# Gated MLP of a transformer block on one core: z1 and z2 made in three column chunks instead of four, and the last block of the output product in two matmuls instead of three

## The chip, the cores and the metric

The kernel runs on one core of one Trainium2 chip. The metric is the time of one execution on the device in microseconds (us); where several runs are given, their median. The profile is one execution of the same program taken by the hardware profiler.

## The reference, cut to what matters

```python
x = A_x                                            # (1, 2048, 512)
h = x + attention(layernorm(x), wqkv, wo)          # 32 heads of 16
z = gelu(layernorm(h) @ w_in)                      # (1, 2048, 1376), tanh form of gelu
z1 = z[..., :688]
z2 = layernorm(z[..., 688:])
g = einsum("ts,bsf->btf", w_sp, z2) + b_sp         # w_sp is 2048 x 2048
out = h + (z1 * g) @ w_out                         # w_out is 688 x 512
```

All inputs and outputs are float32.

## The kernel before, in words

**Precision.** Most matrix products are made of numbers split in two parts: hi is the number rounded to the TensorE's fp32r format, lo is the rest. `mm3` (L92) makes one product block from three matmuls: hi by hi (L93), hi by lo (L94), lo by hi (L95). In each the first operand after the accumulator is stationary (its weight load is PEld in the profile), the second is streamed, one column after another.

**Stages.** (1) Projections and row maxima of the scores, then attention, to about 1407 us of the span. (2) The middle stage, L931 to L972, one row block of 128 rows after another, in the order `h_rows`. (3) The spatial product `w_sp @ z2` with its quarters combined to save products, first half at L1018 to L1126. (4) The last stage, L1196 to L1262, two row blocks in each round `p`: the rest of the spatial product, the gate, and the product with `w_out`.

**The order of work.** From L866 on every engine runs its instructions in the order in which the program writes them; nothing is moved by a scheduler. An instruction waits for the semaphores of what it reads and for the release of what it overwrites.

**A row block of the middle stage (rows `row[k]`).** PE first makes h of row block k+2 (`make_h`, 12 matmuls of 512 columns, L614), then turns the normalised h of row block k+1 (`turn`, four transposes, L882). Then it makes z of row block k: `make_z(sb, i, c)` (L891) makes one chunk of 344 columns in an accumulator of one PSUM bank (five of them rotate) with four `mm3` over the contraction, so 12 matmuls with the transposed h as stationary operand and `w_in` streamed; ScalarE then applies gelu from the accumulator to z (L898). There are four chunks: z2 left, z2 right, z1 left, z1 right (L951, L954, L960, L961). Between them stand `split_o` (L953: the attention output for row block k+3 is split, ScalarE and VectorE), the statistics of z2 (L956, after the second chunk), and the normalised h of row block k+2 (L959, ScalarE, behind the second chunk's gelu). `gate_z` (L900) stores z1 (L904), finishes the statistics, normalises z2 (L909), stores it (L910), and for the second half of the rows forms the sums that stage 3 needs on GpSimd (on VectorE for the last row block). The z1 tile has one buffer, the z2 tile five.

**The product with `w_out` in the last stage.** The gated rows `pr` (128 x 688) must be transposed to serve as stationary operand. 688 is five blocks of 128 and one of 48. `FB` (L39) starts the sixth block at column 560, so it overlaps the fifth; the rows of its weights that were already used are zero (the memset at L1106 and the loading DMA at L1107). `Out.turn` (L1171) makes six transposes (L1176) into PSUM and splits them in two groups of three blocks: hi on ScalarE (L85), lo on VectorE (L90). `Out.multiply` (L1180) then runs `mm3` for each of the six blocks: 18 matmuls of 512 columns for each of the 16 row blocks. The weights `wu` are split at L1128 to L1135.

Of the kernel before, what the change touches and what calls it, by code (L numbers as in the profile page):

```python
# [8 lines left out]
F32 = mybir.dt.float32  # L9
F32R = mybir.dt.float32r  # L10
BF = mybir.dt.bfloat16
I32 = mybir.dt.int32
AF = mybir.ActivationFunctionType
# [5 lines left out]
P = 128  # L19
# [16 lines left out]
FIRST = 1  # L36
RG = 64
VW = DH + 1
FB = [min(i * P, FH - P) for i in range(6)]  # L39
FC = FH // 2  # L40
PITCH = FC + 8
LOW = -3.0e38


@with_exitstack
def block_kernel(ctx: ExitStack, tc: tile.TileContext, x, wqkv, wo, w_in, w_sp4, b_sp, w_out, out):
# [820 lines left out]
    with ExitStack() as mid:  # L867
        m2 = mid.enter_context(tc.tile_pool(name="mid_2", bufs=2))
        zs, zst = {}, {}
        hT = wc.tile([P, 2, 2, DB, P], F32R, name="hT", tag="w2")  # L870
        ph = mid.enter_context(tc.tile_pool(name="mid_ph", bufs=1, space=PSUM))
        pt = mid.enter_context(tc.tile_pool(name="mid_pt", bufs=2, space=PSUM))
        ps = mid.enter_context(tc.tile_pool(name="mid_ps", bufs=5, space=PSUM))

        turned = [0]

        def turn(sb):

            hn = hns.pop(sb)
            tp = pt.tile([P, DB, P], F32, name="tp")  # L880
            for d in range(DB):
                nc.tensor.transpose(tp[:, d, :], hn[:, d * P:(d + 1) * P], ident)  # L882
            hTs[sb] = [hT[:, i, turned[0] % 2] for i in range(2)]
            turned[0] += 1
            split(hTs[sb][0], hTs[sb][1], tp, "act")

        def new_z(sb):
            zs[sb] = [m2.tile([P, FH], F32, name=f"z{i}", bufs=1 + 4 * i) for i in range(2)]
            zst[sb] = m2.tile([P, 2, 6], F32, name="zst")

        def make_z(sb, i, c):  # L891

            hT, f = hTs[sb], slice(i * FH + c * FC, i * FH + (c + 1) * FC)
            acc = ps.tile([P, 512], F32, name="acc")
            for d in range(DB):
                mm3(acc[:, :FC], hT[0][:, d, :], hT[1][:, d, :],
                    wi2[0][:, d, f], wi2[1][:, d, f], d == 0, d == DB - 1)
            nc.scalar.activation(zs[sb][i][:, c * FC:(c + 1) * FC], acc[:, :FC], AF.Gelu_apprx_tanh)  # L898

        def gate_z(sb, meanwhile):  # L900

            z = zs.pop(sb)
            rows = slice(sb * P, (sb + 1) * P)
            nc.scalar.dma_start(z_scr[0][rows, :], z[0])  # L904
            mv = m2.tile([P, 2], F32, name="zmv")
            nc.vector.bn_aggr(mv, zst.pop(sb))
            rs = rstd_of(m2, mv[:, 1:2], 1)
            nb = minus_mean(m2, mv, rs)
            nc.scalar.activation(z[1], z[1], AF.Identity, bias=nb, scale=rs)  # L909
            nc.scalar.dma_start(z_scr[1][rows, :], z[1])  # L910
            zs[sb] = z[1]
            meanwhile()
            if sb < HB:
                return

            k = sb - HB
            el = "pool" if k < HB - 1 else None
            e = nc.gpsimd if el else nc.vector
            (b11, b12), (b21, b22) = ((t[:, :FC], t[:, FC:]) for t in (zs.pop(k), zs.pop(sb)))
            t2 = m2.tile([P, FC], F32, name="t2", bufs=1)  # L920
            e.tensor_sub(b11, b12, b11)
            e.tensor_sub(b12, b22, b12)
            e.tensor_sub(t2, b22, b11)
            put_t = lambda n, t: parts(T[n][0][:, k, :], T[n][1][:, k, :], t, el, el)
            put_t("t3", b12)
            put_t("t2", t2)
            put_t("t1", b11)
            e.tensor_sub(b11, b21, t2)
            put_t("n4", b11)

        w = [Slot(wc, f"w{i}") for i in range(3)]  # L931
        row = dict(enumerate(h_rows))
        turn(row[0])
        for k in range(NB):
            sb, new = row[k], row.get(k + 2)
            if new is not None:
                make_h(new, (ph if k else ps).tile([P, 512], F32, name="acc"))
            if k + 1 < NB:
                turn(row[k + 1])
            if new is not None:  # L940
                mv, rs = scale_h(new)
                nb = minus_mean(e2, mv, rs)
            if k == NB - 3:
                s3 = difference(a11, a21, nc.gpsimd)
                sums(0, a11, a21, a22, nc.gpsimd)
            if k == NB - 2:
                ops = {"s3": put(w[0], s3)}
            if k == NB - 1:
                a21_next = ask(1, 0, 1, "hn")
            new_z(sb)  # L950
            make_z(sb, 1, 0)  # L951
            if k + 3 < NB:
                split_o(row[k + 3])  # L953
            make_z(sb, 1, 1)  # L954
            for c in range(2):
                nc.vector.bn_stats(zst[sb][:, c, :], zs[sb][1][:, c * FC:(c + 1) * FC])  # L956
            if new is not None:
                hns[new] = e2.tile([P, D], F32, name="hn", bufs=3)
                nc.scalar.activation(hns[new], xrs.pop(new), AF.Identity, bias=nb, scale=rs)  # L959
            make_z(sb, 0, 0)  # L960
            make_z(sb, 0, 1)  # L961
            hTs.pop(sb)
            gate_z(sb, lambda: k + 4 < NB and load_o(row[k + 4]))
            if not k:
                invert()
            if k == NB - 5:
                a21, a22 = ask(1, 0, 0, "rc"), ask(1, 1, 0, "o")
            if k == NB - 4:
                a11 = ask(0, 0, 0, "xr")
            if k == NB - 2:  # L970
                ops["s2"] = put(w[1], a11)
        ops["a22"] = put(w[2], a22)  # L972
# [3 lines left out]
    with ExitStack() as fin:  # L976
# [41 lines left out]
        for p in range(HB):  # L1018
# [67 lines left out]
            if not last:  # L1086
                nxt["s1"] = put(new[3], a21)
                if ahead:
                    a21 = a
                else:  # L1090
                    a11 = a
                b = load_b(0, 0, p + 1)
                if not ahead:
                    asked = [(1, 1, k) for k in range(HB)] + [(1, 0, k) for k in range(HB)]
                    bs = [load_b(*asked.pop(0)) for _ in range(8)]
            else:
                a12 = put(f[2], a22)
                b21 = [quarter(zc, "b21", f"t2_{i}") for i in range(2)]
                for k in range(HB):
                    put_next(b21, k)  # L1100
                for i in (4, 5):
                    t = e2.tile([P, D], F32, name="wr", tag="rc")
                    r0 = i * P - FB[i]
                    if r0:

                        nc.gpsimd.memset(t, 0.0)  # L1106
                    nc.sync.dma_start(t[r0:], w_out[i * P:FB[i] + P, :])  # L1107
                    raw_u.append(t)
            product(g4, ops["a22"], T["n4"])
            if p == HB - 2:  # L1110
# [21 lines left out]
        for i, places in enumerate([[w[:, 2 * i:2 * i + 2, :] for w in wu] for i in range(2)]  # L1132
                                   + [[w[:, 4, :] for w in wu], [t[:, j * D:(j + 1) * D] for j in range(2)]]):
            parts(*places, raw_u[i])
        wu = [[w[:, i, :] for i in range(5)] + [t[:, j * D:(j + 1) * D]] for j, w in enumerate(wu)]  # L1135
        late.close()

# [26 lines left out]
        class Out:  # L1164
# [5 lines left out]

            def turn(self, *groups):  # L1171
                if self.pT is None:
                    self.pT = [f2.tile([P, len(FB), P], F32R, name=f"pT{i}") for i in range(2)]
                    self.tp = ps_t.tile([P, 8, P], F32, name="tp")
                for i in range(groups[0][0], groups[-1][1]):
                    nc.tensor.transpose(self.tp[:, i, :], self.pr[:, FB[i]:FB[i] + P], ident)  # L1176
                for i0, i1 in groups:
                    split(self.pT[0][:, i0:i1, :], self.pT[1][:, i0:i1, :], self.tp[:, i0:i1, :], "act")

            def multiply(self, blocks, end=True):  # L1180
                first = self.acc is None
                if first:
                    self.acc = ps_o.tile([P, 512], F32, name="acc")
                for i in blocks:
                    mm3(self.acc, self.pT[0][:, i, :], self.pT[1][:, i, :], wu[0][i], wu[1][i],
                        first and i == blocks[0], end and i == blocks[-1])

            def store(self, pieces=1):
                y = f2.tile([P, D], F32, name="y")
# [6 lines left out]
        for p in range(HB):  # L1196
# [21 lines left out]
            if p and not last:  # L1218
                a11 = put(f[0], nxt[1][0])
            if prev:  # L1220
                prev.multiply(range(len(FB)))
            product(g3, s4, b22, halves[0])
            if prev:
                prev.store()
# [6 lines left out]
                combine(nc.vector, nxt[1][2], nxt[1][1], nxt[1][2], ALU.subtract)  # L1231
                s4 = put(f[1], nxt[1][2])
            if p and not last:
                bot.multiply(range(len(FB)))
            product(g2, a12, b21, halves[0] if p else range(HB - 2))
            if p and not last:
                bot.store()
# [4 lines left out]
            product(g2, a12, b21, halves[1] if p else range(HB - 2, HB))  # L1242
            if not p:
                a11 = put(f[0], nxt[1][0])
                bot.multiply(range(len(FB)))
            nc.vector.tensor_add(left, g2, left)
            (nc.vector if last else nc.gpsimd).tensor_mul(left, left, z1[0][:, :FC])
            if not p:
# [5 lines left out]
                bot.store()  # L1254
            prev = top

        bot.multiply(range(len(FB)))
        prev.turn((0, 3))
        prev.multiply(range(3, 6), False)
        bot.store()  # L1260
# [31 lines left out]
```

## Time and profile before

| | |
|---|---|
| median of 3 runs | 1869.95 us (1868.23, 1869.95, 1870.05) |
| the profiled execution's own time | 1869.55 us |
| its span, first to last instruction | 1867.8 us |
| granted TensorE clock | 1.000 |
| busy: PE, VectorE (DVE), ScalarE (ACT), GpSimd (POOL) | 1857.6, 1526.0, 1318.7, 225.6 us |

The time of the profiled execution is 1.75 us longer than its span; that part lies around the instructions. In the profile PE is TensorE matmul, PEld its weight load, SP the engine that issues most DMAs. `L93` is line 93 of the kernel before. A group line gives line, engine, operation, what is written and read, shapes and count, then total busy time in us, and the mean duration of one in ns. The duration of a matmul in the records is longer than its share of the engine, because matmuls overlap in the pipeline; the share is the distance from one start to the next. The chain of waits is followed back from the last instruction, at each step to what released it.

### The profile page before, as it was taken

To read this page: it belongs to the slowest core of one execution; us is meant where nothing else is said; L and a number is where in the kernel's file an instruction comes from. 1 tells how busy PE (TensorE), PEld (TensorE's weight loads), DVE (VectorE), ACT (ScalarE), POOL (GpSimd) and SP (SyncE) were. 2 spreads that over 40 slices of the span, in tenths; PEclk is the share of its full clock that TensorE was granted. 3 is DMA by queue.
4 is the path that set the end of the run, shared out by engine and by line. 5 is a ranking of instruction groups with operands and counts; after the bars stand their busy time and mean duration, and the time that the engine had idled before them with its cause. 6 is when DMAs were issued, how large, how long until landed. Compare 5 with 4: busy or idle time off the path is not lost.

```text
span 1867.8 us, 32350 instructions
## 1 busy us (share of the span) xinstructions
PE 1857.6 (99%) x11606; PEld 1061.9 (57%) x11606; DVE 1526.0 (82%) x3044; ACT 1318.7 (71%) x1696; POOL 225.6 (12%) x304
## 2 busy tenths in 40 slices
PE   8999999999999999999999999999999999999999
PEld 6776444444444444444444444444438999999998
DVE  6487999999999999999999999999936666877654
ACT  3224888888888888888888888888895444434221
POOL 2241000011010100000000000000001756001111
PEclk9999999999999999999999999999999999999999
DMA  5688111221120211021011011100114555768562
GB/s 187 179 204 201 41 24 30 47 54 28 39 56 16 52 41 25 15 49 39 13 38 37 19 34 44 25 14 14 33 52 124 163 163 167 226 188 272 190 190 87
DMA packets 148680, 159.82 MB, mean 86 GB/s; under 512 B 63080, under 2 KB 93304, under 8 KB 147176
## 3 DMA queue, kind: packets, MB, share of 16 engines
q1 hardware_dynamic: 143736, 146.35, 29.4%
q10 hardware_dynamic: 4752, 11.41, 1.6%
q8 instruction: 91, 1.49, 0.3%
q14 instruction: 69, 0.57, 0.1%
q0 software_dynamic: 32, 0.01, 0.0%
HBM read 101.16 MB, written 55.61 MB: 84 GB/s over the span
## 4 chain that ended last, share of the span: by engine, by line
PE 99%; DVE 1%; ACT 0%; DMA 0%; issue 0%; SPq 0%; DVEq 0%; ACTq 0%
PE pv L681 27%; PE m L222 26%; PE s L670 13%; PE acc L93 6%; PE acc L95 6%; PE acc L94 6%; PE g L95 4%; PE g L94 4%; PE g L93 4%; PE acc L614 2%; PE tp L1176 1%; PE h L614 0%; PE tp L882 0%; PE tp L366 0%; PE tp L222 0%; ACT xT L85 0%
## 5 line engine op out<-in xcount | busy, mean ns | idle before, releaser
L673 ACT ACTIVATE pt<-s 128x1024 f32<-128x1024 f32 x1024 | 994.3, 1030 | 141.4 <-PE s L670 136.5
L227 DVE TENSOR_REDUCE mx<-m 128x1 f32<-128x512 f32 x1508 | 956.1, 683 | 99.6 <-PE m L222 57.2
L222 PE MATMUL m<-kst,qst 48*128 48x512 f32 x1508 | 604.3, 447 | 0.0
L681 PE MATMUL pv<-pt,vst 128*32 128x512 f32 x4096 | 545.9, 605 | 0.0
L670 PE MATMUL s<-qst,kst 50*128 50x512 f32 x2048 | 464.9, 428 | 0.0
L222 PEld LDWEIGHTS m<-kst,qst 48*128 48x128 f32 x1508 | 262.3, 184 | 316.4 <-DVE mx L227 221.9
L670 PEld LDWEIGHTS s<-qst,kst 50*128 50x128 f32 x2048 | 222.4, 185 | 54.0 <-ACT pt L673 29.6
L222 PE MATMUL m<-uvs,qst 48*128 48x512 f32 x497 | 246.6, 496 | 0.0
L222 PEld LDWEIGHTS m<-uvs,qst 48*128 48x128 f32 x497 | 90.8, 183 | 205.4 <-DVE mx L227 204.6
L681 PEld LDWEIGHTS pv<-pt,vst 128*32 128x32 f32 x4096 | 80.7, 108 | 157.9 <-issue 155.1
L236 DVE CUSTOM_DVE_ANT_0 ab<-m,ab 128x512 f32<-128x512 f32 x249 | 169.1, 679 | 0.0
L232 ACT ACTIVATE ab<-m 128x512 f32<-128x512 f32 x248 | 149.3, 602 | 4.1 <-PE m L222 4.0
L87 POOL CAST mparts<-nm 128x16 fp32r<-128x16 f32 x32 | 6.3, 198 | 882.3 <-DVE nm L242 882.3
L822 ACT ACTIVATE ws<-a 128x512 fp32r<-128x512 f32 x80 | 45.8, 621 | 53.4 <-PE g L95 27.1
L93 PE MATMUL acc<-wi,hT 128*128 128x344 f32 x256 | 83.1, 325 | 0.0
L95 PE MATMUL acc<-wi,hT 128*128 128x344 f32 x256 | 81.7, 319 | 0.0
L94 PE MATMUL acc<-wi,hT 128*128 128x344 f32 x256 | 81.7, 319 | 0.0
L898 ACT ACTIVATE z<-acc 128x344 f32<-128x344 f32 x64 | 29.2, 457 | 62.8 <-PE acc L95 62.7
L823 DVE TENSOR_TENSOR ws<-a,ws 128x512 fp32r<-128x512 f32 x80 | 56.3, 745 | 13.4 <-ACT ws L822 13.3
L93 PE MATMUL g<-b,ws 128*128 128x344 f32 x192 | 62.6, 326 | 0.0
L85 ACT ACTIVATE part<-acc 128x512 fp32r<-128x512 f32 x32 | 19.1, 598 | 60.9 <-PE acc L95 54.3
L95 PE MATMUL g<-t,ws 128*128 128x344 f32 x192 | 61.3, 319 | 0.0
(196 smaller groups left out, 2164.1 us busy)
## 6 DMA issues: line engine op xcount, KB each, us to landing
a<-in_w_sp SPq DMA_DIRECT2D x80, 256.0 KB
qst<-q_scr SPq DMA_DIRECT2D x192, 64.0 KB
z_scr<-z ACTq DMA_DIRECT2D x32, 344.0 KB
kst<-k_scr SPq DMA_DIRECT2D x42, 256.0 KB
k_scr<-part SPq DMA_DIRECT2D x16, 512.0 KB
q_scr<-part SPq DMA_DIRECT2D x16, 512.0 KB
z<-z_scr SPq DMA_DIRECT2D x14, 344.0 KB
b<-z_scr SPq DMA_DIRECT2D x24, 172.0 KB
```

The lines of the kernel that those rows point to most:

```text
L93: nc.tensor.matmul(ps, lh, rh, start=first, stop=False)
L94: nc.tensor.matmul(ps, lh, rl, start=False, stop=False)
L95: nc.tensor.matmul(ps, ll, rh, start=False, stop=last)
L222: nc.tensor.matmul(acc, q[r, p, c], keys[r, p], start=True, stop=True)
L227: nc.vector.reduce_max(at(t, e if t else e - 1), acc, axis=AX.X)
L232: nc.scalar.activation(ab[0], acc, AF.Abs)
L236: nc.vector.tensor_tensor_reduce(ab[0], acc, ab[0], 0.5, LOW, ALU.add, ALU.max, at(0, 0))
L670: nc.tensor.matmul(s[:, t, :], k[r, p, kb * P:(kb + 1) * P], q[r, p, :], start=True, stop=True)
L673: nc.scalar.activation(t, s, AF.Exp, scale=DH ** -0.5)
L681: nc.tensor.matmul(pv[0][32 * j:32 * j + 32, :], vst[hg % 2][:, c:c + 32], pts[j % 2][:, j // 2, :], start=kb == 0, stop=kb == NB - 1)
L822: nc.scalar.activation(hi, src, AF.Copy)
L823: (nc.gpsimd if el == "pool" else nc.vector).tensor_sub(lo, src, hi.bitcast(F32))
```

## The change

Two parts. **z in three chunks:** for all row blocks but the last, z1 and z2 are taken as one matrix of 1376 columns and made in chunks of columns 912 to 1376, 464 to 912 and 0 to 464 (464, 448 and 464 columns). The middle chunk holds the first 224 columns of z2 and the last 224 of z1 and gets one gelu for each. The last row block keeps four chunks of 344. The statistics of z2, and the normalised h of row block k+2, stay behind the second chunk. **The last block of the `w_out` product:** the sixth transposed block (columns 560 to 688, of which the last 64 serve) gets hi in its lower 64 partitions as before, and VectorE writes the lo part of these into the upper 64 partitions. The sixth block of the weights holds the 48 rows twice, once for each half; the upper half of its lo part is zeroed by GpSimd. So two matmuls (with hi and lo of the weights) make what three made.

```diff
-FB = [min(i * P, FH - P) for i in range(6)]
+NF = 5
+FL = FH - P // 2
+ZC = [(912, 1376), (464, 912), (0, 464)]
+ZL = [(FC * i, FC * i + FC) for i in (2, 3, 0, 1)]
...
-        def make_z(sb, i, c):
+        def make_z(sb, c0, c1):
-            hT, f = hTs[sb], slice(i * FH + c * FC, i * FH + (c + 1) * FC)
+            hT, f = hTs[sb], slice(c0, c1)
             acc = ps.tile([P, 512], F32, name="acc")
             for d in range(DB):
-                mm3(acc[:, :FC], hT[0][:, d, :], hT[1][:, d, :],
+                mm3(acc[:, :c1 - c0], hT[0][:, d, :], hT[1][:, d, :],
                     wi2[0][:, d, f], wi2[1][:, d, f], d == 0, d == DB - 1)
-            nc.scalar.activation(zs[sb][i][:, c * FC:(c + 1) * FC], acc[:, :FC], AF.Gelu_apprx_tanh)
+            for i in (1, 0):
+                a, b = max(c0, i * FH), min(c1, i * FH + FH)
+                if a < b:
+                    nc.scalar.activation(zs[sb][i][:, a - i * FH:b - i * FH], acc[:, a - c0:b - c0],
+                                         AF.Gelu_apprx_tanh)
...
-            make_z(sb, 1, 0)
+            chunks = ZC if k + 1 < NB else ZL
+            make_z(sb, *chunks[0])
             if k + 3 < NB:
                 split_o(row[k + 3])
-            make_z(sb, 1, 1)
+            make_z(sb, *chunks[1])
...
-            make_z(sb, 0, 0)
-            make_z(sb, 0, 1)
+            for c in chunks[2:]:
+                make_z(sb, *c)
...
                     t = e2.tile([P, D], F32, name="wr", tag="rc")
-                    r0 = i * P - FB[i]
-                    if r0:
+                    if i < NF:
+                        nc.sync.dma_start(t, w_out[i * P:i * P + P, :])
+                    else:
                         nc.gpsimd.memset(t, 0.0)
-                    nc.sync.dma_start(t[r0:], w_out[i * P:FB[i] + P, :])
+                        for r0 in (NF * P - FL, NF * P - FL + P // 2):
+                            nc.sync.dma_start(t[r0:r0 + FH - NF * P], w_out[NF * P:, :])
...
+        nc.gpsimd.memset(places[1][:P // 2].bitcast(F32), 0.0)
...
                 for i0, i1 in groups:
-                    split(self.pT[0][:, i0:i1, :], self.pT[1][:, i0:i1, :], self.tp[:, i0:i1, :], "act")
+                    hi, lo, tp = self.pT[0], self.pT[1], self.tp
+                    nc.scalar.activation(hi[:, i0:i1, :], tp[:, i0:i1, :], AF.Copy)
+                    i1 = min(i1, NF)
+                    nc.vector.tensor_sub(lo[:, i0:i1, :], tp[:, i0:i1, :], hi[:, i0:i1, :].bitcast(F32))
+                if i >= NF:
+                    h = P // 2
+                    nc.vector.tensor_sub(hi[:h, NF, :], tp[h:, NF, :], hi[h:, NF, :].bitcast(F32))
...
                 for i in blocks:
-                    mm3(self.acc, self.pT[0][:, i, :], self.pT[1][:, i, :], wu[0][i], wu[1][i],
-                        first and i == blocks[0], end and i == blocks[-1])
+                    if i < NF:
+                        mm3(self.acc, self.pT[0][:, i, :], self.pT[1][:, i, :], wu[0][i], wu[1][i],
+                            first and i == blocks[0], end and i == blocks[-1])
+                        continue
+                    for j in range(2):
+                        nc.tensor.matmul(self.acc, self.pT[0][:, i, :], wu[j][i], start=False,
+                                         stop=end and i == blocks[-1] and j == 1)
```

The other lines of the diff only replace `len(FB)` by `NF + 1`.

More of the change, by code (lines that the diff above doesn't have):

```diff
@@ L1172, in turn @@
                 if self.pT is None:
-                    self.pT = [f2.tile([P, len(FB), P], F32R, name=f"pT{i}") for i in range(2)]
+                    self.pT = [f2.tile([P, NF + 1, P], F32R, name=f"pT{i}") for i in range(2)]
                     self.tp = ps_t.tile([P, 8, P], F32, name="tp")
                 for i in range(groups[0][0], groups[-1][1]):
-                    nc.tensor.transpose(self.tp[:, i, :], self.pr[:, FB[i]:FB[i] + P], ident)
+                    c = min(i * P, FH - P)
+                    nc.tensor.transpose(self.tp[:, i, :], self.pr[:, c:c + P], ident)
                 for i0, i1 in groups:
-                    split(self.pT[0][:, i0:i1, :], self.pT[1][:, i0:i1, :], self.tp[:, i0:i1, :], "act")
+                    hi, lo, tp = self.pT[0], self.pT[1], self.tp
[5 more added lines that the diff above has]
+                    nc.vector.tensor_sub(hi[:h, NF, :], tp[h:, NF, :], hi[h:, NF, :].bitcast(F32))
             def multiply(self, blocks, end=True):
@@ L1220, in block_kernel @@
             if prev:
-                prev.multiply(range(len(FB)))
+                prev.multiply(range(NF + 1))
             product(g3, s4, b22, halves[0])
@@ L1233, in block_kernel @@
             if p and not last:
-                bot.multiply(range(len(FB)))
+                bot.multiply(range(NF + 1))
             product(g2, a12, b21, halves[0] if p else range(HB - 2))
@@ L1244, in block_kernel @@
                 a11 = put(f[0], nxt[1][0])
-                bot.multiply(range(len(FB)))
+                bot.multiply(range(NF + 1))
             nc.vector.tensor_add(left, g2, left)
@@ L1255, in block_kernel @@
             prev = top
-        bot.multiply(range(len(FB)))
+        bot.multiply(range(NF + 1))
         prev.turn((0, 3))
```

## The prediction

> **What bounds the kernel now.** First the page, for the engine that carries the end; then the chain of waits in order of time, for the pace of the two stages that change; then PE's timeline, start by start, for the price of one matmul. From the page:
>
> ```profile
> span 1867.8 us, 32350 instructions
> PE 1857.6 (99%) x11606; PEld 1061.9 (57%) x11606; DVE 1526.0 (82%) x3044; ACT 1318.7 (71%) x1696; POOL 225.6 (12%) x304
> ...
> PE 99%; DVE 1%; ACT 0%; DMA 0%; issue 0%; SPq 0%; DVEq 0%; ACTq 0%
> ```
>
> The chain is PE to 99%. Busy time alone would not prove a dense PE, so here is the chain of waits over the middle and last stages (start, us, what):
>
> ```profile
> 1421.41 2.77 PE acc L614 x12
> 1424.19 0.44 PE tp L882 x4
> 1432.17 2.78 PE acc L614 x12
> ...
> 1453.69 2.78 PE acc L614 x12
> ...
> 1550.53 2.77 PE acc L614 x12
> ```
>
> Row blocks of the middle stage follow each other at 1432.17 - 1421.41 = 10.76 us, and at 1550.53 still in that step (12 steps from 1421.41 are 129.1 us): PE alone sets the pace, other engines only have to keep up. Both parts of the change take matmuls from PE in such stages, so the question is what a matmul costs PE, and whether an engine that feeds it becomes late.
>
> PE's timeline (start, us, engine, line, what), where the record's own length, 0.32 or 0.39, is no price because records overlap; the price is start to start. A row block's z, then in the last stage a spatial product, six transposes, a second half, a `w_out` product:
>
> ```profile
> 1424.38 0.41 PE L93 MATMUL acc<-wi,hT 128*128 128x344 f32 x1
> 1424.62 0.32 PE L94 MATMUL acc<-wi,hT 128*128 128x344 f32 x1
> ...
> 1432.01 1.32 PE L614 MATMUL acc<-wo,o 128*128 128x512 f32 x5
> ```
> ```profile
> 1794.69 0.31 PE L94 MATMUL g<-b,ws 128*128 128x344 f32 x1
> ...
> 1798.29 0.82 PE L1176 MATMUL tp<-ident,pr 128*128 128x128 f32 x6
> ...
> 1800.82 0.39 PE L93 MATMUL acc<-wu,pT 128*128 128x512 f32 x1
> ...
> 1802.90 0.39 PE L93 MATMUL acc<-wu,pT 128*128 128x512 f32 x1
> ...
> 1804.26 0.39 PE L93 MATMUL acc<-wu,pT 128*128 128x512 f32 x1
> ...
> 1804.72 0.40 PE L95 MATMUL acc<-wu,pT 128*128 128x512 f32 x1
> 1804.95 0.32 PE L93 MATMUL g<-b,ws 128*128 128x344 f32 x1
> ```
>
> From 1794.69 to the transposes stand 23 matmuls of 344 columns: 3.60 us, 156.5 ns each. The 18 of the `w_out` product take 4.13 us, but not evenly: the first nine 2.08 us (231.1 ns each), the next eight, 1802.90 to 1804.72, 1.82 us (227.5 ns). One group in the last round shows the floor (17 intervals in 3.85 us, 226.5 ns):
>
> ```profile
> 1855.37 0.39 PE L93 MATMUL acc<-wu,pT 128*128 128x512 f32 x1
> ...
> 1859.22 0.40 PE L95 MATMUL acc<-wu,pT 128*128 128x512 f32 x1
> ```
>
> So 168 more columns cost 226.5 - 156.5 = 70.0 ns, 0.4167 ns a column, and 156.5 - 344 x 0.4167 = 13.2 ns belong to the matmul, however wide. Some bursts of 512 columns add about 4.6 ns to each of their first nine. These three numbers carry the forecast.
>
> **The `w_out` part.** Sixteen `Out.multiply` groups go from 18 matmuls to 17. The one that goes is at the end of the group, where the pace is 227 ns: 16 x 0.227 = **3.6 us**. It is on the path: PE runs from one row above to the next without a gap. What the part adds, with its cover:
>
> - VectorE: the second lo group has 256 columns instead of 384, and one subtraction of 64 partitions x 128 columns follows. The rows:
>
> ```profile
> L90 DVE TENSOR_TENSOR pT<-tp,pT 128x384 fp32r<-128x384 f32 x32 | 17.8, 558 | 34.1 <-ACT pT L85 33.9
> L1192 DVE TENSOR_TENSOR y<-acc,h 128x512 f32<-128x512 f32 x15 | 10.3, 685 | 2.3 <-PE acc L95 2.3
> ...
> L1192 DVE TENSOR_TENSOR y<-acc,h 128x256 f32<-128x256 f32 x2 | 0.8, 420 | 2.4 <-PE acc L95 2.4
> ```
>
>  From 420 and 685 ns a column costs 1.035 ns, so 256 columns 0.42 and 128 columns 0.29 us: 0.71 instead of 0.56, 0.15 us more a turn. Its bounds are 0 (as if free) and 0.56 (as 384 columns). I take 0.29 and cost it at nothing, because PE reads the sixth block last:
>
> ```profile
> 1800.84 0.56 DVE L90 TENSOR_TENSOR pT<-tp,pT 128x384 fp32r<-128x384 f32 x1 [0.56 <-ACT pT L85]
> 1801.31 1.53 DVE L1211 SCALAR_TENSOR_TENSOR pr<-g,bias,q 128x344 f32<-128x344 f32 x3
> ```
>
>  The new subtraction would end near 1800.84 + 0.71 = 1801.55; PE comes to the sixth block at 1804.26, so 2.7 us of cover. Behind it in VectorE's queue the three gates (1801.31) slip by 0.15 us, and with them GpSimd's product for the next transposes:
>
> ```profile
> 1802.60 1.67 POOL L1215 TENSOR_TENSOR pr<-pr,z 128x688 f32<-128x688 f32 x1 [4.46 <-DVE pr L1211]
> ...
> 1806.84 0.82 PE L1176 MATMUL tp<-ident,pr 128*128 128x128 f32 x6
> ```
>
>  That product ends at 1804.27 and is wanted at 1806.84; with PE 0.23 us earlier and GpSimd 0.15 later 2.2 us are left.
> - Once per kernel: a memset of 64 x 512 on GpSimd (bounded by 0 and the 0.53 us of the memset of 128 x 512 at 1684.34 below), and one more DMA issue of 48 rows on SP:
>
> ```profile
> 1684.34 0.53 POOL L1106 MEMSET wr<- 128x512 f32 x1 [111.59 <-DVE ws L823]
> 1705.70 0.92 POOL L1229 TENSOR_TENSOR pr<-pr,qz 128x344 f32<-128x344 f32 x1 [20.83 <-DMA a<-in_w_sp]
> ...
> 1692.81 0.90 SPq L1107 DMA_DIRECT2D wr<-in_w_out x2
> ```
>
>  GpSimd is idle for 20.8 us around it. SP's later issues slip by about 0.45 us, half of the pair's 0.90; the loads behind it are for the stage after, where no row of the waits names a DMA on PE. Nothing.
>
> **The z part.** In 15 row blocks 48 matmuls of 344 columns become 24 of 464 and 12 of 448; the columns are the same. Now: 1424.38 to 1432.01, 7.63 us, of which the first matmul after the transposes has 0.24 (0.085 more than its kind; it stays). After: 24 x (13.2 + 464 x 0.4167 = 206.6) + 12 x (13.2 + 448 x 0.4167 = 199.9) = 7.36, plus 0.085, plus the burst's extra. That last term is unknown for these widths. If no matmul has it: 7.44 us, 0.19 saved. If all 36 have 4.6 ns: 7.61, 0.02 saved. A loss is excluded by these rows: no column is added, and the widest matmul in them already costs no more than that. I take the burst as the `w_out` group shows it, 9 x 4.6 = 0.04: 7.48, 0.15 saved. Over 15 row blocks **2.2 us** (0.3 to 2.8).
>
> The Trainium skill gives another price: "TensorE: Matmul & The Clock Gate", section "Back-to-back issue gap", gives a warm matmul by itself N/2.4 and a fixed 2.5 ns. Its slope is that of the rows, its fixed part is not: it makes 145.8 ns of 344 columns, where the trace has 156.5. By it the 180 matmuls that go would be worth 0.45 us in all, and the time would lie in the first rival below.
>
> What the z part moves on the other engines, by a row block as it is now:
>
> ```profile
> 1443.45 0.33 ACTq L904 DMA_DIRECT2D z_scr<-z  x1
> ...
> 1449.95 0.46 ACT L898 ACTIVATE z<-acc 128x344 f32<-128x344 f32 x1 [0.92 <-PE acc L95]
> 1450.31 0.80 ACT L959 ACTIVATE hn<-xr,nb,rs_r 128x512 f32<-128x512 f32 x1
> 1451.83 0.46 ACT L898 ACTIVATE z<-acc 128x344 f32<-128x344 f32 x1 [0.72 <-PE acc L95]
> ```
> ```profile
> 1445.73 0.69 DVE L624 TENSOR_TENSOR xr<-acc,xr 128x512 f32<-128x512 f32 x1 [2.35 <-PE acc L614]
> ...
> 1449.74 0.68 DVE L90 TENSOR_TENSOR o<-o,o 128x512 fp32r<-128x512 f32 x1
> ```
>
> The first chunk will end 0.6 us later in its row block (12 x 206.6 for 12 x 156.5 ns), the second 1.1 us later (with 12 x 199.9). So the second chunk's first gelu starts near 1451.1 instead of 1449.95, two gelus of 224 columns take at most 0.46 us each, and the normalised h (L959) ends by 1452.8. PE wants it for transposes behind the next 12 matmuls of L614, in the chain at 1453.69 + 2.78, less 0.3 for the earlier row block and the 0.16 by which the chain's starts stand after the timeline's (1432.17 against 1432.01): 1456.0. **Cover 3.2 us**; gone, the excess would count in full in each row block. `split_o`'s second half now ends at 1450.42; 0.7 us later it is still 2.2 us ahead of the product that reads it. The statistics and the normalising of z2 come 1.1 us later; behind them in VectorE's queue stands the next sum of h (L624), which VectorE reaches 2.35 us early today, so it stays on time. All of it at nothing.
>
> **The sum.** 3.6 + 2.2 = 5.8 us. The profiled execution took 1869.55, its span 1867.8 and 1.75 around it that stay: 1869.55 - 5.8 = **1863.7 us**. It stands 0.4 below the median of 1869.95, so against the median the ratio is -0.31% to -0.33%.
>
> **The rivals.**
>
> 1. *A matmul's price goes by its columns.* If the extra 4.6 ns stays on all wide matmuls of the middle stage, where L614's 12 take 2.78 us (231 ns each) without ever reaching 226.5, the z part gives 0.3 us; if it goes by a line through 157.1 ns (7.54 us of the chain over 48) and 231, 5.6 ns fixed, 1.0 us. 1869.55 - 3.6 - (0.3 to 1.0) = 1864.9 to 1865.6. For it: the middle stage's only 512-column matmuls are all of this kind. Against it: the pace falls back after nine in the `w_out` group.
> 2. *The hand-over of the sixth block.* PE waits at each group for the new VectorE subtraction and gives the matmul back: only the z part stays, 1867.3. Against it: 2.7 us of cover, worn out only if a 0.29 us instruction comes 2.7 us late.
> 3. *The single z1 buffer (slower).* z1 is now overwritten from the second chunk on, not the third. Between the issue of a row block's z1 store (1443.45) and the next row block's first write (1451.83) lie 8.4 us; after the change 7.7, as the write moves to near 1451.5 and the store's issue some 0.1 us back. If the store has not landed, ScalarE waits, L959 behind it, and PE's transposes behind that. The time to landing isn't shown, but bounded: gelus wait for PE alone today, so it is under 8.4.
>
> ```profile
> ACT z L898 <- PE acc L95: 61.3, 55, 1.4
> ```
>
>  With 3.2 us of cover PE is touched only by stores of over 10.9 us, and the change ends slower than before from 11.3 us on (15 x 0.39 is the 5.8 gained); at 11.5 us it would be 1863.7 + 15 x 0.6 = 1872.7. Today's bound speaks against it; for it, only that the stores start at other moments between the loads.
> 4. *It does not do what it says.* The changed program's order holds 540 wide and 48 of 344 columns for z, and 272 matmuls with `wu`: it does.
>
> **How the numbers follow.** The forecast 0.70 (1862.7 to 1864.6), rival 1 0.15, rival 2 0.06, rival 3 0.05, unlisted 0.04. Less than 0.2%, 3.7 us, is about what a measurement of this kernel can tell from no change; runs of one kernel differ by 1.8 us. Faster by over 0.2% means under 1866.2: 0.69 from the forecast and 0.11 from rival 1, whose upper end is near that line, 0.80. Same: 0.01 + 0.04 + 0.06 + 0.01 = 0.12. Slower: 0.05 + 0.03 = 0.08. The range, 1861.8 to 1866.4, holds the forecast and rival 1 with 0.9 us for the difference of runs, and leaves out the rest, some 0.18.
>
> **What the next profile would show.** z matmuls of 464 columns 207 ns start to start, of 448 200 ns (211 and 204 by rival 1); row blocks at 10.61 us instead of 10.76; `w_out` groups at 3.90 instead of 4.13 us; no wait of PE on VectorE or ScalarE. A gap before the sixth block would be rival 2, a gelu waiting for a DMA rival 3. Wrong altogether: a row block no shorter than 10.74.

## The result and the profile after

The changed kernel takes 1863.76 us (median of 11 runs, 1863.55 to 1865.5), the kernel before 1868.13 us (11 runs, 1867.66 to 1870.05): a ratio of 0.9978, 95% interval 0.997 to 0.9986, 4.4 us less. The forecast of 1863.7 us is met almost to the digit, and that is in part luck: the profiled execution from which it starts, 1869.55 us, turned out 1.4 us above the median of its kernel, and the gain was put at 5.8 us. The two errors cancel. The direction and the two parts hold; their sizes need a closer look.

The page of the changed kernel, profiled in an execution of 1863.55 us (line numbers of the changed kernel are 3 to 25 higher; `mm3` is now L96 to L98):

```profile
span 1861.7 us, 31964 instructions
PE 1852.8 (100%) x11410; PEld 1047.3 (56%) x11410; DVE 1530.4 (82%) x3060; ACT 1317.8 (71%) x1696; POOL 225.7 (12%) x305
...
PE 98%; DVE 1%; issue 0%; ACT 0%; DMA 0%; SPq 0%; POOL 0%; POOLq 0%; DVEq 0%; ACTq 0%
```

PE still carries the end. To see where the 6.1 us between the two spans are, take PE's timeline at four places: the first matmul of h in the middle stage, the first of the spatial product, the first of a `w_out` group, the last. Of the kernel before:

```profile
1410.41 0.94 PE L614 MATMUL acc<-wo,o 128*128 128x512 f32 x3
...
1576.66 0.32 PE L93 MATMUL g<-t,ws 128*128 128x344 f32 x1
...
1708.92 0.39 PE L93 MATMUL acc<-wu,pT 128*128 128x512 f32 x1
...
1863.68 0.39 PE L95 MATMUL acc<-wu,pT 128*128 128x512 f32 x1
```

Of the changed kernel:

```profile
1408.77 0.47 PE L617 MATMUL acc<-wo,o 128*128 128x512 f32 x1
...
1573.80 0.32 PE L96 MATMUL g<-t,ws 128*128 128x344 f32 x1
...
1706.06 0.39 PE L96 MATMUL acc<-wu,pT 128*128 128x512 f32 x1
...
1857.56 0.39 PE L98 MATMUL acc<-wu,pT 128*128 128x512 f32 x1
```

| stage | before | after | difference |
|---|---|---|---|
| up to the middle stage | 1410.41 | 1408.77 | -1.64 |
| middle stage | 166.25 | 165.03 | **-1.22** |
| spatial product, first half | 132.26 | 132.26 | 0 |
| last stage | 154.76 | 151.50 | **-3.26** |

The first line is no gain: its code is the same in both, and single profiles of it differ by this much (1408.77 to 1410.41 us). The middle stage gave 1.2 us where 2.2 were forecast, the last stage 3.3 where 3.6 were.

**Middle stage.** The chain of waits, row block by row block (start, us, what):

```profile
1419.71 2.76 PE acc L617 x12
...
1547.83 2.76 PE acc L617 x12
```

Twelve row blocks take 128.12 us, 10.677 each; before 10.76. PE's timeline shows one of them:

```profile
1433.34 0.46 PE L96 MATMUL acc<-wi,hT 128*128 128x464 f32 x1
1433.64 0.37 PE L97 MATMUL acc<-wi,hT 128*128 128x464 f32 x1
...
1435.95 0.37 PE L96 MATMUL acc<-wi,hT 128*128 128x448 f32 x1
...
1438.39 0.37 PE L96 MATMUL acc<-wi,hT 128*128 128x464 f32 x1
...
1440.90 0.86 PE L617 MATMUL acc<-wo,o 128*128 128x512 f32 x3
```

After the first matmul's 0.30 us, eleven of 464 columns take 2.31 us (210 ns each), twelve of 448 2.44 us (203 ns), twelve of 464 2.51 us (209 ns). The floor was put at 206.6 and 199.9 ns; no chunk's mean comes down to it.

**Last stage.** PE waits twice where it did not, or less, before. PE's timeline in round 1 and in the last round; the bracket gives what PE waited for:

```profile
1714.62 0.40 PE L97 MATMUL acc<-wu,pT 128*128 128x512 f32 x1
1715.25 0.50 PE L98 MATMUL acc<-wu,pT 128*128 128x512 f32 x1 [0.23 <-DVE pT L1194]
...
1846.82 0.32 PE L98 MATMUL g<-b,ws 128*128 128x344 f32 x1
1847.46 0.55 PE L1189 MATMUL tp<-ident,pr 128*128 128x128 f32 x3 [0.32 <-POOL pr L1254]
```

Of the kernel before, at the same two places:

```profile
1717.11 0.55 DVE L90 TENSOR_TENSOR pT<-tp,pT 128x384 fp32r<-128x384 f32 x1
1717.74 0.40 PE L94 MATMUL acc<-wu,pT 128*128 128x512 f32 x1
1717.98 0.40 PE L95 MATMUL acc<-wu,pT 128*128 128x512 f32 x1
...
1852.76 0.32 PE L95 MATMUL g<-b,ws 128*128 128x344 f32 x1
1853.11 0.55 PE L1176 MATMUL tp<-ident,pr 128*128 128x128 f32 x3
```

From L97 to L98 are 0.63 us instead of 0.24, and the matmul after it is 0.1 us late too: 0.5 us. From the last L98 to the transposes are 0.64 us; before it were 0.35 at this place: 0.29 us. What stands behind them is in VectorE's timeline of the same kernel:

```profile
1712.84 1.29 DVE L826 TENSOR_TENSOR ws<-a,ws 128x512 fp32r<-128x512 f32 x2
1714.04 0.69 DVE L1217 TENSOR_TENSOR y<-acc,h 128x512 f32<-128x512 f32 x1
1714.64 0.55 DVE L1194 TENSOR_TENSOR pT<-tp,pT 128x384 fp32r<-128x384 f32 x1
...
1845.13 0.42 DVE L1194 TENSOR_TENSOR pT<-tp,pT 128x256 fp32r<-128x256 f32 x1 [0.56 <-ACT pT L1192]
1845.57 0.29 DVE L1198 TENSOR_TENSOR pT<-tp,pT 64x128 fp32r<-64x128 f32 x1
1845.89 0.52 DVE L1253 TENSOR_TENSOR pr<-g,pr 128x344 f32<-128x344 f32 x1
```

At 1714 VectorE works through a queue without a gap (no bracket, no idle time): it is behind there, and PE's third matmul waits for the end of L1194. At 1845 the new subtraction (L1198; it writes lo into partitions 0 to 63, the half that the section on the change calls the upper one) stands between a lo group and L1253, whose result GpSimd multiplies before PE can transpose it: L1253 starts 0.76 us after the second lo group did. In the kernel before it was 0.47:

```profile
1851.07 0.56 DVE L90 TENSOR_TENSOR pT<-tp,pT 128x384 fp32r<-128x384 f32 x1 [0.56 <-ACT pT L85]
1851.54 0.50 DVE L1228 TENSOR_TENSOR pr<-g,pr 128x344 f32<-128x344 f32 x1
```

So the edit costs VectorE 0.29 us at this turn, not 0.15. The durations were forecast well (0.42 and 0.29); what was left out is that before, the next instruction started 0.09 us ahead of the end of the lo group (1851.07 + 0.56 is later than 1851.54), while here each starts 0.02 to 0.03 us behind the end of the one before. Why these two do not run into each other was not looked for.

### The profile page after: what moved, and what is told of

It is laid out like the page before. It is cut to its first block, busy times and chain, and to the rows that moved or that the text cites. A ratio compares the mean times of both kernels' runs of the same rounds, so it can differ in the third digit from the quotient of the medians.

```text
span 1861.7 us, 31964 instructions
## 1 busy us (share of the span) xinstructions
PE 1852.8 (100%) x11410; PEld 1047.3 (56%) x11410; DVE 1530.4 (82%) x3060; ACT 1317.8 (71%) x1696; POOL 225.7 (12%) x305
## 4 chain that ended last, share of the span: by engine, by line
PE 98%; DVE 1%; issue 0%; ACT 0%; DMA 0%; SPq 0%; POOL 0%; POOLq 0%; DVEq 0%; ACTq 0%
PE pv L684 27%; PE m L225 26%; PE s L673 13%; PE acc L96 5%; PE acc L98 5%; PE acc L97 5%; PE g L98 4%; PE g L97 4%; PE g L96 4%; PE acc L617 2%; PE tp L1189 1%; PE h L617 0%; PE tp L885 0%; PE acc L1210 0%; PE tp L369 0%
## 5 line engine op out<-in xcount | busy, mean ns | idle before, releaser
L904 ACT ACTIVATE z<-acc 128x464 f32<-128x464 f32 (+2 forms) x64 | 27.6, 456 | 65.3 <-PE acc L98 63.3
L96 PE MATMUL acc<-wi,hT 128*128 128x464 f32 (+2 forms) x196 | 72.8, 371 | 0.0
L98 PE MATMUL acc<-wi,hT 128*128 128x464 f32 (+2 forms) x196 | 71.8, 366 | 0.0
L97 PE MATMUL acc<-wi,hT 128*128 128x464 f32 (+2 forms) x196 | 71.6, 365 | 0.0
L96 PE MATMUL g<-b,ws 128*128 128x344 f32 x192 | 62.6, 326 | 0.0
L98 PE MATMUL g<-t,ws 128*128 128x344 f32 x192 | 61.3, 319 | 0.0
```

The lines of the kernel that those rows point to most:

```text
L96: nc.tensor.matmul(ps, lh, rh, start=first, stop=False)
L97: nc.tensor.matmul(ps, lh, rl, start=False, stop=False)
L98: nc.tensor.matmul(ps, ll, rh, start=False, stop=last)
```

## The experiments

Theories: **A**, each part has its price, the wide matmuls keep an extra of 3 to 5 ns throughout, and the new waits belong to the `w_out` part; **B**, the extra dies out after some nine matmuls, as forecast; **C**, the new waits come from the middle stage ending earlier; **D**, the extra comes from widths; **E**, from addresses; **F**, from the order of the instructions.

### The z part alone

```diff
 (kernel before)
-            make_z(sb, 1, 0) ... make_z(sb, 0, 1)
+            chunks = ZC if k + 1 < NB else ZL    # and make_z by columns
```

> Only the z part (chunks of 464, 448 and 464 columns), the w_out product as before with 18 matmuls a group. Theory A (each part has its own price, and the wide matmuls keep most of their extra of 3 to 5 ns through the whole row block): row blocks of 10.68 us instead of 10.76, 1.2 us less in the middle stage, about 1866.9 beside 1868.1 of before, and no new wait of PE in the last stage. Theory B (the forecast's size, the extra only in the first nine matmuls): 10.61 us, 2.2 us less, 1865.9. Theory C (the two new waits of the last stage come from the middle stage ending earlier, with loads that do not): the waits of PE for VectorE in round 1 (0.4 us) and for GpSimd in the last round (0.29 us) show here too, and the gain is 0.5 us or less.

Measured: 1866.88 us beside 1867.97 of before, ratio 0.9995 (0.9986 to 1.0004), 1.1 us less. Row blocks of 10.677 us (12 in the 128.12 us between these rows of the chain), and among PE's waits in the last stage only those that were there before:

```profile
1420.05 2.76 PE acc L616 x12
...
1548.17 2.76 PE acc L616 x12
```
```profile
PEld tp L1183 <- POOL pr L1236: 0.3, 1, 0.3
PEld acc L97 <- DVE pT L92: 0.2, 1, 0.2
```

(The kernel before has the same two waits, of 0.3 and 0.2 us.) A's size, and C falls: the middle stage is as short as in the changed kernel, 165.03 us, and no new wait appears. By itself this part is not told apart from no change by the times; the row blocks show it. The last stage, whose code is that of before, takes 154.46 us here and 154.76 in the profile before: such a stage differs by 0.3 us between single profiles.

### The w_out part alone

```diff
 (changed kernel)
-            chunks = ZC if k + 1 < NB else ZL
+            chunks = ZL
```

> Only the w_out part, z in four chunks of 344 columns in all row blocks. Theory A: the middle stage as before (10.76 us a row block), the last stage 3.2 us shorter, with both new waits of PE in it (for VectorE's lo part in round 1, for GpSimd's product in the last round), about 1864.9 beside 1868.1. Theory C: the new waits are gone and the last stage is 4.0 us shorter, 1864.1.

Measured: 1865.39 us, ratio 0.9986 (0.9977 to 0.9994), 2.6 us less. PE's waits in the last stage (engine, line, what it waited for, us, times, longest):

```profile
PEld acc L98 <- DVE pT L1194: 0.8, 2, 0.6
PEld tp L1189 <- POOL pr L1254: 0.6, 1, 0.6
PE tp L1189 <- POOL pr L1254: 0.3, 1, 0.3
PE acc L98 <- DVE pT L1194: 0.2, 1, 0.2
```

Both new waits are here: they belong to this part. Its last stage takes 151.62 us, 3.1 less than in the profile before and 2.8 less than in that of the z part alone; the median moved 0.5 less than A had it. The two parts alone gain 1.1 and 2.6 us, 3.7 together; the changed kernel gained 4.4, and 4.0 when it was timed again (below). The stage up to the middle one differs by up to 1.6 us between single profiles of the same code, so medians some tenths apart are not followed further.

### Other widths

```diff
-ZC = [(912, 1376), (464, 912), (0, 464)]
+ZC = [(896, 1376), (480, 896), (0, 480)]
```

> As the changed kernel, with chunks of 480, 416 and 480 columns. The fixed price of a matmul is the same for any width, so 36 matmuls should cost the same for any split of 1376 columns. Theory A (the extra belongs to the middle stage, not to the width): row blocks of 10.68 us as with 464, 448 and 464, and the same time, 1863.8. Rival D (the extra comes from widths that do not fit a step of 32 columns, as 344 and 464 do not, and 448, 480, 416 and 512 do): row blocks near 10.60 us, 1.1 us less, 1862.7.

Measured: 1864.16 us, ratio 0.9982 (0.9973 to 0.9991). Row blocks of 10.697 us:

```profile
1420.95 2.76 PE acc L617 x12
...
1549.31 2.76 PE acc L617 x12
```

Rival D falls: widths in steps of 32 columns make the row block 0.02 us longer, not 0.08 shorter. (A chunk of 512 columns, the width that does come down to its floor in the `w_out` groups, was not tried for z.)

### Every chunk twice

```diff
-            for d in range(DB):
+            for d in list(range(DB)) * 2:
                 mm3(acc[:, :c1 - c0], ...
```

Each z chunk is computed twice over, so its time is not the changed kernel's.

> As the changed kernel, and the 12 matmuls of each z chunk run twice over, the second time from a cleared accumulator, so that PE has twice the matmuls on the same data with no wait between. For its start-to-start distances alone; the time is worth nothing. Theory A (the extra stays as long as the middle stage's wide matmuls run): the 24 of a chunk of 464 columns at 209 to 211 ns throughout. Theory B (a burst that dies out when PE runs on without a wait): 211 ns in the first ten of a chunk, 206.7 in the others. Row blocks 7.4 to 7.6 us longer, the whole about 1863.8 + 15 x 7.45 + 7.5 = 1983 us.

Measured: 1983.81 us. PE's timeline of a third chunk, whose 24 matmuls of 464 columns run without a wait:

```profile
1440.68 0.37 PE L96 MATMUL acc<-wi,hT 128*128 128x464 f32 x1
...
1443.19 0.38 PE L96 MATMUL acc<-wi,hT 128*128 128x464 f32 x1
...
1445.71 2.91 PE L617 MATMUL acc<-wo,o 128*128 128x512 f32 x12
```

The first twelve take 2.51 us, the second twelve 2.52: in these chunks nothing dies out. Theory B, the step on which the forecast's z part rests, falls. The row block's twelve matmuls of 512 columns are another case: taken singly in the changed kernel's trace, they start 224 to 236 ns apart eight times and then 227, so the burst of the `w_out` groups does occur in this stage and ends there too. What the z chunks show is something else. In the middle chunk the second twelve distances repeat the first twelve within 1 ns (197 to 208 ns, means over the row blocks), in the third chunk they do not: the operands count, and what was issued before them as well.

### The weights at other addresses

```diff
+    gap(ec, 64)          # 32, 128, 256 in the others
     wi2 = [ec.tile([P, DB, 2 * FH], F32R, name=f"wi{i}") for i in range(2)]
```

Only the address of the streamed `w_in` moves (with what lies behind it in its pool); no instruction is added or reordered on PE. The first was made with the changed kernel, the others with the variant below.

> The changed kernel with the w_in weights 64 bytes further on in memory, the widths and the order as they are. Theory E (the extra of 3 to 5 ns of a wide matmul is in the addresses of what is streamed and what is loaded as weights): another pattern of distances within a row block and another mean than 210.0 and 202.7 ns. Theory F (it is in the order of the instructions and their widths): the same pattern to 1 or 2 ns, 10.68 us a row block.

> The variant without the two new waits, and the w_in weights 32 bytes further on, so that all chunks of what is streamed start on a multiple of 64 bytes, while the transposed h stays 32 bytes off one (so far both are 32 off). In the kernel before, the chunks of 344 columns that start so have 1.1 ns of extra on the mean and those 32 off -0.15. Theory E (addresses set the extra): row blocks clearly other than 10.68, by these signs longer, 10.70 or more. Theory F (order and widths): 10.68.

> As both_s32 with 128 bytes, so 32 off a multiple of 64 as in the changed kernel. Theory E: another pattern within the row block and a length between 10.49 (no extra at all) and 10.70. Theory F: 10.68.

> As both_s32 with 256 bytes. Theory E: another pattern, between 10.49 and 10.70. Theory F: 10.68. The shortest of this call and of shift64 (10.645) is then timed.

The chain of waits over the same twelve row blocks, of the shifts by 64, 32 and 256 bytes in this order:

```profile
1420.63 2.73 PE acc L618 x12
...
1548.37 2.73 PE acc L618 x12
```
```profile
1420.69 2.77 PE acc L618 x12
...
1549.49 2.77 PE acc L618 x12
```
```profile
1419.94 2.76 PE acc L618 x12
...
1548.07 2.76 PE acc L618 x12
```

| shift, bytes | row block, us | 464 and 448 columns, mean ns | one execution, us |
|---|---|---|---|
| 0 | 10.677 | 210.0, 202.7 | |
| 32 | 10.733 | 211.2, 204.2 | 1865.19 |
| 64 | 10.645 | 210.0, 202.6 | 1864.07 |
| 128 | 10.708 | 210.6, 203.3 | 1863.32 |
| 256 | 10.677 | 210.0, 202.7 | 1863.66 |

(The means are of the start-to-start distances in 15 row blocks, without the first of each; the shift of 64 has the two waits in the last stage, the others not.) The row block's length depends on the address, and 256 bytes further on it is that of no shift again, also distance by distance within the row block. So F falls, as the instructions, widths and order are the same in all, and E has a part. It is a small part: the four addresses move the mean of 464 columns by 1.2 ns, and at none does it come nearer to the floor than 3.4 ns. Where the bulk of the extra comes from stays open. With 64 bytes the twelve matmuls of h take 2.73 us instead of 2.76, though their own operands did not move: singly, their burst ends after two matmuls instead of eight. That is nearly the whole gain of this shift, and it shows that what a matmul costs depends also on those before it.

### z1's columns first

```diff
-ZC = [(912, 1376), (464, 912), (0, 464)]
+ZC = [(0, 464), (464, 912), (912, 1376)]    # statistics of z2 behind the third chunk
```

> The changed kernel with the chunks in the order 0 to 464, 464 to 912, 912 to 1376, the statistics of z2 behind the third. Theory E (addresses): the columns keep their price, so the chunk 0 to 464 has a mean of 209.4 ns in first place and the chunk 912 to 1376 about 211.0 in third, each with its own pattern. Theory F (place in the row block): the first chunk has 211.0 and the third 209.4, whichever columns they are.

Measured: chunk 0 to 464 in first place 209.9 ns on the mean (209.3 in third place), chunk 912 to 1376 in third place 211.0 (210.8 in first). The columns keep their price within 0.6 ns, where F had them trade it: against F again. The row block takes 10.657 us, and yet the one execution 1865.74: z2's statistics now come too late for the stage that follows, whose first half takes 133.73 us instead of 132.26:

```profile
1581.70 0.32 PE L98 MATMUL g<-t,ws 128*128 128x344 f32 x1
1582.81 0.42 PE L96 MATMUL g<-n,ws 128*128 128x344 f32 x1 [0.79 <-ACT ws L825]
```

### The two waits taken away, and the best version

```diff
-            if not last:
+            if p and not last:
                 a12 = put(f[2], nxt[1][1])
             if not p:
+                late12 = nxt[1][1]
                 bot.store()
...
             nc.scalar.activation(left, g1, AF.Identity, bias=bt)
+            if p == 1:
+                a12 = put(f[2], late12)
...
-            nc.gpsimd.tensor_mul(right, right, z1[0][:, FC:])
+            (nc.vector if last else nc.gpsimd).tensor_mul(right, right, z1[0][:, FC:])
```

> The changed kernel with its two new waits of PE taken away: the split of round 1's a12 operand (ScalarE and VectorE) moves from the end of round 0 to behind the gates of round 1, so that VectorE's queue is 1.3 us shorter where round 1 turns its rows; and in the last round the product of the right half with z1 is VectorE's (0.52 us) instead of GpSimd's (0.92). Theory A (the waits are VectorE's added subtraction, 0.26 to 0.29 us a turn, and PE's own earlier arrival, at two places without cover): the 0.40 us wait in the third matmul of round 1's first w_out group and the 0.29 us one ahead of the last round's three transposes go, about 0.8 us less: 1863.0. Rival (VectorE is late by its load, whatever the order): a wait of the same size shows at another place, 1863.8.

> The changed kernel unaltered, for a comparison on the same chip with the variant without the two waits: 1863.8, 4.2 us below before.

Measured on one chip: 1863.53 us (1863.23 to 1864.21) with the two edits, 1864.09 (1863.77 to 1865.55) for the changed kernel, beside 1868.05 of before; ratios 0.9976 (0.9967 to 0.9985) and 0.9978 (0.9969 to 0.9987). Of the 0.8 us 0.56 show in the medians, though the intervals of the two ratios overlap; in the traces the last stage takes 150.74 us instead of 151.55. PE's waits in the last stage:

```profile
PEld tp L1189 <- issue: 0.2, 1, 0.2
PEld acc L98 <- DVE pT L1194: 0.2, 1, 0.2
```

Both waits are gone and none has taken their place; the rival (VectorE late by its load) falls. With the weights 64 bytes further on as well:

> The variant without the two new waits, with the w_in weights 64 bytes further on, the best of the addresses tried. Theory E (the distances repeat with the address modulo 256 bytes and do not depend on the last stage): row blocks of 10.645 us as in shift64, 15 x 0.032 = 0.5 us less than the variant without the shift: 1863.1, and 0.9 us less than the changed kernel on the same chip by its earlier pair of 1864.1 and 1863.5.

Measured: 1863.13 us (1862.95 to 1863.63) beside 1867.94 of before, ratio 0.9975 (0.9965 to 0.9984), 4.8 us less. It is below both kernels; that the last 0.4 us over the variant without the shift are real rests on the row block's 0.032 us in the trace (15 of them are 0.5), as the two were timed on different occasions.

## Why the prediction was right, and where it was not

- **What bounds the kernel:** right. PE carried 99% of the chain, and what was taken from PE showed in the time.
- **The price of a matmul, 13.2 ns beside its columns:** right as a floor, and in the last stage met: `w_out` groups of 17 take 3.86 us where no burst is in them (226.6 ns from start to start).
- **"I take the burst as the `w_out` group shows it, 9 x 4.6 = 0.04":** the term that was mis-sized. In the z chunks an extra stays throughout, 3.4 ns for 464 and 2.8 for 448 columns on the mean, against the 0.7 ns that those of 344 had (157.2 against 156.5). A row block saves 0.083 us, not 0.15, the part 1.2 us, not 2.2. The line through the middle stage's own two prices, rival 1, had said 1.0, and its prices for 464 and 448 columns, 5.6 ns and 0.44 a column, are the measured means to 0.3 ns. It was the better guide to the size; its reason is not shown by that. It rests on L614's matmuls "without ever reaching 226.5", read from a row that merges twelve; taken singly in the trace before, they have the burst, and the eleventh costs 227. The shifts of address show besides that columns alone do not set the price.
- **3.6 us of `w_out`:** right on PE's own account, then changed by two things that were not forecast. Several groups of the profiled execution run without the burst of 0.044 us that 14 of the 16 had before, which in this profile is another 0.39 us (with the wait of round 1 left out); the two waits take back 0.79. -3.63 - 0.39 + 0.79 = -3.23, seen -3.26. The 0.39 is not to be credited to the change: the z part alone, with the groups of 18, lacks the burst in several groups too, and its last stage is 0.3 us shorter for it.
- **"2.7 us of cover" and "2.2 us are left":** the first is right in all sixteen groups, as nothing in the trace ever waits for the new subtraction (L1198). The second is right in round 5, from which it was read, and in the other middle rounds, where PE has no such wait; it is wrong in the last. The step that failed is "cost it at nothing" for VectorE: cover was shown for one product in one round, and the delay of what else stands in VectorE's queue was not priced. Round 0 makes operands that the other rounds spread differently, so that VectorE enters round 1 with a full queue. Counted from the first matmul with `wu`, its lo group in round 1 ends 0.39 us later than before (9.13 for 8.74), of which 0.26 is the longer split in round 0, and PE's second matmul comes 0.26 us earlier (8.56 for 8.82). Of these 0.65 us only 0.26 were cover: the third matmul started 0.32 us behind the end of the lo group, now 0.06. The rest, 0.39, is the wait, and 0.1 falls on the matmul behind. In the last round the three transposes already waited for GpSimd's product, 0.35 us from the last start, so any delay ahead of that product counted in full. Rival 2 had the right engine but the wrong instruction: PE never waited for the sixth block.
- **z1's single buffer, rival 3:** did not happen. In the middle stage ScalarE's gelus wait for PE, and a single time 2.0 us for GpSimd, which PE didn't notice; no DMA is named.

```profile
ACT z L904 <- POOL z L928: 2.0, 1, 2.0
```

- **The rule of the Trainium skill** ("TensorE: Matmul & The Clock Gate", section "Back-to-back issue gap"), 2.5 ns of fixed cost: its 0.45 us for the z part lie 0.8 below the measured 1.2, and the forecast's 2.2 lies 1.0 above. The fixed part measured here is 13.2 ns.
- **The base:** one profiled execution was 1.4 us above the median of its kernel. That does not matter for a ratio, but it decided whether the absolute time was met.

## What to carry to other kernels

Price a matmul from start-to-start distances, taken singly, in the very stage that is changed; a row that merges twelve hides a burst. A fixed cost and a slope from another stage give a floor, and an extra that is a transient there may be lasting here. Cover has to be read at the tightest place where an edit is repeated (first and last rounds above all), not at a typical one: an engine whose timeline shows no idle time ahead of the edit has little (0.26 us in round 1). And when PE is made faster, its readers' waits must be looked up again, because the time saved and the time added meet at the same spot.

## What the runs showed of the hardware

- A matmul of 128 x 128 weights in fp32r costs N columns at 0.4167 ns and 13.2 ns (156.5 ns at 344, 226.5 at 512), and in z's chunks 0.7 to 4.7 ns more on the mean (157.2 at 344 columns; 211.2 at 464 with a shift of 32 bytes). A small part of that depends on the address of the streamed operand, with the same distances at 0 and 256 bytes, and on the matmuls before; 32 bytes changed a row block of 48 such matmuls by 0.057 us. What in the memory or the engine makes the rest was not found.
- In the `w_out` groups the burst of nine slow matmuls comes or does not come, with the same program: a second profile of the changed kernel has it in one group more (3.90 us instead of 3.86 for the fifteenth). It was not settled what starts it.
- After four transposes the first matmul takes 0.085 us more than the others, at 344 as at 464 columns (0.24 and 0.295 us).
